# A fused spectral filter and gated MLP on one core: the forward token transform from fp16 halves, an opening with fp32 transposes, and a re-timed planner

## The chip, the cores and the metric

The kernel runs on one core of a Trainium2 chip. Its engines are PE (TensorE: matmuls; its weight loads are shown apart, as PEld), DVE (VectorE), ACT (ScalarE), POOL (GpSimd) and SP (SyncE, which issues the transfers). The metric is the device time of one execution in microseconds. The kernel before takes 434.8 us, the median of three runs (433.99 to 435.23).

## The reference

The input `x` has 2048 tokens of 448 features. Two branches read its layer norm, and both are added to `x`:

```python
xn = layernorm(x)                            # over the 448 features
A  = irfft2(rfft2(xn) * (w_r + 1j * w_i))    # over tokens and features
g  = relu(xn @ W_gate)                       # 448 -> 1792
B  = (g * (xn @ W_up)) @ W_down              # 1792 -> 448
return x + A + B
```

All of it is fp32. The kernel multiplies in fp16 and keeps the precision by splitting a number in a high and a low half (`hi = fp16(a)`, `lo = fp16(a - hi)`); a product then takes three matmuls, hi·hi, hi·lo and lo·hi.

## The kernel before

**The MLP.** The 1792 hidden features are 14 tiles f of 128, taken in three groups of 5, 5 and 4; the tokens are four chunks q of 512 (order 0, 2, 1, 3). `gu_unit(f, q)` makes gate and up of one tile and chunk: 20 matmuls of 128x512 and two of half the rows, from the weight halves `wt` and the transposed layer norm `T`. Behind it `gu_post` runs `gu_relu` (ACT), `gu_times` (DVE, the instruction g<-gu,g), `gu_hi` (ACT) and `gu_lo` (DVE, h<-g,h). After all tiles of a group and chunk, `dn_mm` multiplies h by W_down (128x448 matmuls into the banks dn). These two are the stream of PE. Two pairs of PSUM banks serve the gu units by turns, so DVE has about one unit's time, after the unit's last matmul, to read its bank.

**The weights.** A tile of W_gate/W_up is loaded (wst<-in_wgu), squared and summed on ACT (junk<-wst), summed over the partitions on POOL (wm), turned into a power of two on DVE (eg, wsc), and split into wt: the high half on ACT (`w_hi`), the low half on DVE (`w_lo`).

**The spectral branch** is the background, listed in `bg` with a DVE cost for each step. Forward, in eight passes: `f_dft` (features; 48 small matmuls), an eviction by ACT, `f_fold`, `f_a` and `f_b` (butterflies on DVE over a buffer in the tile arena), `f_sdft` (tokens: a 64-point transform by four fp32 matmuls of 64x64 weights and 464 columns, one in each quadrant of PE's array, L824), an eviction `f_y`, and `f_y1`. Then come butterflies over the tiles y (`stage2` to `stage4`), the multiplication by the filter, and the way back, whose runs on PE are `i_sdft` and `i_ddft`. A background run uses PE in another form than the stream does.

**The opening.** For chunk 0 the layer norm has to be transposed on PE before anything else can start. `ln_xn` makes xn in fp32; `ln_hi` (ACT) and `ln_lo` (DVE) split it into halves; `ln_tp` transposes three 128x128 tiles of each half, for four token tiles; `ln_ev` evicts them to T (rows 0 to 2 high, 5 to 7 low); `ln_tpc` transposes the remaining 64 features in 24 pieces for the rows 3, 4 and 8. While the data comes, `keep_warm` runs matmuls on zeros (16, and 4 more later). Chunks 2, 1 and 3 are transposed by DMA.

**The order.** Every call is recorded by `Order` and placed by `Order.place` (all instructions therefore carry the line L416 of the profile). The opening is fixed by hand: each engine takes its own pieces in the order of the string OPENING (L34). From there on `place` picks for each engine, by a table of costs (`cost`, `matmul`, `dma`, ISSUE, SLACK, SOON), among the nodes that are ready; the stream keeps its order, and a background run is put in when it is ready and has waited longer than its hold (HOLDS, L28), or when the stream's next matmul is not ready. An instruction of DVE counts as free for a dependent one at its end plus 0.04 us, and the engine for another one 0.083 us ahead of its end (ISSUE). `run_bg` gives the background out over the units from RAMP to LASTGU before the last, and BACK says how many units early it may start.

Of the kernel before, what the change touches and what calls it, by code (L numbers as in the profile page):

```python
# [34 lines left out]
lx0 lx4 bn0 lx12 bn4 lx8 lw ag0 lid lw ag4 sqA raA rbA rcA warm rdA rmA xn0 bn12 bn8 an4 ag12 hi0 ag8 lo0 hi4 sqB tpA0  # L35
wsqW0g0 lx14 lw tpB0 raB lo4 rbB rcB tpB4 kw4 rdB rmB aevA0 wsqW0g1 lw xn8 tpA4 parW0g0 wexW0g0 lx6 lw vevB4 hi8 vevB0
hi12 wscW0g0 vevA4 whiW0g0 lx10 tpA8 aevA8 tpA12 parW0g1 lo8 tpB8 wsqW1g1 hh00 hl00 wsqW1g0 lw lw lw xn12 vevA12 hh01
lo12 wexW0g1 wloW0g0 parW1 wscW0g1 tpB12 whiW0g1 vevB12 lx2 tpC aevC1 bn6 lwd3 lh01 lh00 wexW1 wscW1 vevB8 hh10 vevC0
whiW1g0 wloW0g1 hl10 wloW1g0 whiW1g1 wloW1g1 hl11 bn10 bn2 bn14 hh11 lwd0 wsqW3g1 ml0 ml1 wsqW2g0 wsqW2g1 lh11 wsqW3g0
parW2 lfd ag2 hl01 ag10 lh10 ag14 ag6 hp0 re0 tm0 lw lwd1 sqC raC wexW2 lw gu1g0 rbC wscW2 rcC rdC xn14 parW3 wexW3  # L40
whiW2g1 wloW2g1 lwd4 gu1g1 hi14 cp14 wscW3 xn2 whiW2g0 lo14 wloW2g0 whiW3g0 hi2 lwd2 whiW3g1 wsqW4g0 xn10 re1 wsqW4g1
parW4 wloW3g0 hi10 cp2 ly0 tm1 gu2g1 gu2g0 cp10 ly4 wdq0 wdq4 wloW3g1 wexW4 gh0 xn6 wdq3 lo10 hp2 gu3g0 hi6 re2 ly12
wscW4 whiW4g0 lo2 whiW4g1 gu3g1 lo6 wdq2 gh1 tm2 dm14 wdq1 gl0 wloW4g0 gu4g0 ly8 dm10 wloW4g1 gl1 cp6 gu4g1 re3 gh2
tm3 wdp wdsc gh3 gl3 aevC2 wdh1 dm2 gl2 wdl1 wdh4 dm6 wdh3 wdl4 hp4 re4 wdl3 tm4 wdh0 wdl0 wdh2 wdl2 gh4 gl4
# [3 lines left out]
LASTGU = 9  # L48
# [56 lines left out]
def _constants():  # L105
# [54 lines left out]
    c_fm = c_fm.reshape(2, 4, 128, 2, 64).transpose(1, 2, 0, 3, 4)  # L160
    ident = np.eye(128, dtype=np.float16)
# [21 lines left out]
class Order:  # L183
# [3 lines left out]
    ISSUE = dict(V=-0.083, A=-0.098, G=-0.06)  # L187
    SOON = 0.2
    SWITCH = 0.093
    SLACK = 0.8  # L190
# [85 lines left out]
    def cost(self, eng, op):  # L276
        name, k, n = op.call[0].__name__, op.call[2], max(op.n)
        if eng == "G":
            return 0.47 + 0.16 * (op.n[0] > 2) * (op.n[0] - 2) if "reduce" in name else 0.2 + 2e-3 * n
        ap = any(c == 1 for c in op.n[1:]) and n > 8  # L280
        if eng == "V":
            return 0.15 + 1.04e-3 * n + 0.06 * ap
        dark = op.out[1].space == bass.MemoryType.PSUM
        return 0.22 + 8e-4 * n - 0.04 * dark + 0.08 * ap + 0.09 * ("accum_out" in k)

    def matmul(self, op):
        o, w, x = op.out
        rows, cols = w.ap[0][1], op.n[1]
        r, c = w.offset // w.ap[0][0], o.offset // o.ap[0][0]
        half = (64, 64 if cols <= 64 else 128) if rows <= 64 else (128, 128)  # L290
        quads = [(i, j) for i in ((0, 1) if rows > 64 or x.dtype == F32 else (r // 64,))
                 for j in ((0, 1) if half[1] == 128 else (c // 64,))]
        return half, quads, 0.42 if x.dtype == F32 else op.n[0] / 2400 + 0.0025

    def dma(self, op):
        o, i = op.out
        if "transpose" in op.call[0].__name__:
            return 1.37, 1.78, 1.55
        z = o.ap[0][1] * op.n[0] * (4 if o.dtype == F32 else 2)
        dram = isinstance(i.tensor, bass.DRamTensorHandle)  # L300
        return 0.47 if dram else 0.63, 2.0 if dram else 1.7, z * 2.8e-6

    def place(self):
# [14 lines left out]
        def lag(op):  # L318
            pe = op.node.eng == "P"
            far = 0.04 if op.node.eng == "S" or op.node.fixed else self.SLACK  # L320
            return max([d.end + (far if d.node.eng == "S" else 0.04) for d in op.deps
                        if not (pe and d.node.eng == "P")], default=0.0)
# [20 lines left out]
        def pick(e):  # L343
# [6 lines left out]
            if e != "P":  # L350
                t = [est(n) for n in r]
                lo = min(t) + self.SOON
# [5 lines left out]
            run = min(runs, key=lambda v: (v[1] > free["P"] + self.SOON, v[0].key)) if runs else None  # L358
# [7 lines left out]
            if self.matmul(head.ops[0])[0][0] == 64 and h[1] <= now + self.SOON:  # L366
                return h
# [53 lines left out]
def tile_gfnet_reglu(ctx: ExitStack, tc: tile.TileContext, x, xr, wgu, wd, wf, ident, c_fd, c_fm, c_im, c_row, c_id,  # L421
                     out):
    nc = tc.nc
    order = Order()
    V, A, P, G, Q = (order.engine(e, eng) for e, eng in zip("VAPGS", (nc.vector, nc.scalar, nc.tensor, nc.gpsimd, nc.sync)))
# [106 lines left out]
    id_t = ft([128, 128], F16, "id_t")  # L532
# [46 lines left out]
    def load_fm(q):  # L579
        t = ft([128, 2, 2, 64], F32, "fm", 4)  # L580
# [55 lines left out]
    for t in tts:  # L636
        G.memset(t[:, 3:9:5, 64:128], 0.0)
# [41 lines left out]
    def ln_lo(n2):  # L679
# [41 lines left out]
    def ln_ev(n2, part, act):  # L721
        q, j = n2 % 4, n2 // 4
        copy(Tq[q][:, 5 * part:5 * part + 3, 128 * j:128 * (j + 1)], tp[n2, part][:, 0:3], act)

    def ln_tpc(q):

        b = (fx(), fx())
        for i in range(3):
            tp["end", i] = b[i // 2].bitcast(F16)[:, 512 * (i % 2):512 * (i % 2) + 512]
        for j in range(4):  # L730
            t = tt[q + 4 * j].rearrange("p a b -> p (a b)")
            c, l = t[:, 384:448], t[:, 1024:1088]
            for i, half in enumerate(((c, t[:, 7:512:8]), (l, c), (l, t[:, 647:1152:8]))):
                for h in range(2):
                    P.transpose(tp["end", i][64 * h:64 * h + 64, 128 * j:128 * j + 128], half[h], id_t)

    def ln_evc(q, i, act):
        copy(Tq[q][:, (3, 4, 8)[i], :], tp["end", i], act)
# [38 lines left out]
    def f_dft(a, b):  # L777

        ps, T = fx2(), Tq[a % 4]
        with order.run(HOLDS[0]):  # L780
# [32 lines left out]
    def f_part(a, n2):  # L813
        k = int(n2 != a)
        return Fq[a][:, :, :, KC * k:KC * (k + 1)].rearrange("p s c k -> p c s k")

    def f_hi(a, n2):
        Xh[n2] = ft([128, 2, 2, NG, KC], F16, "Xh", 2)
        A.activation(Xh[n2][:, 0], f_part(a, n2), AF.Copy)

    def f_lo(a, n2):
        V.tensor_tensor(Xh[n2][:, 1], f_part(a, n2), Xh[n2][:, 0], op=OP.subtract)

    def f_sdft(a):  # L824
        w, ps = fm_t[a], fx2()
        sfx[a] = ps
        with order.run(HOLDS[1]):
            for k in range(2):
                for b in range(2):
                    p, q = slice(64 * k, 64 * k + 64), slice(64 * b, 64 * b + 64)  # L830
                    P.matmul(ps[q, k, 0:XW], w[p, b], f_part(a, a + 8 * b)[p], start=True, stop=True,
                             skip_group_check=True)
# [199 lines left out]
    def row_dft(d):  # L1032
        y = state["rowps"] = fx()[:, 0:NG * KC]
        with order.run(HOLDS[0]):
# [79 lines left out]
    def i_sdft(p):  # L1114
        ps = fx2()
        sps[p] = ps
        with order.run(HOLDS[2]):
# [33 lines left out]
    def i_ddft(a, b):  # L1151
# [6 lines left out]
        with order.run(HOLDS[3]):  # L1158
# [225 lines left out]
    PE_US = {"f_dft": 0.85, "f_sdft": 0.75, "i_sdft": 0.85, "i_ddft": 0.82, "row_dft": 0.2}  # L1384
# [42 lines left out]
    for k, a in enumerate(seq):  # L1427
# [3 lines left out]
        add(2.2, f_b, a)  # L1431
        if k < 7:
# [176 lines left out]
    def keep_warm(n):  # L1609
        for i in range(n):  # L1610
            P.matmul(wps[i % 2], warm[:, 0:128], warm, start=True, stop=True)
# [3 lines left out]
              **{f"kw{n}": (lambda n=n: keep_warm(n)) for n in (4,)},  # L1615
# [6 lines left out]
    for c, q in enumerate(CHUNKS[:2]):  # L1622
# [4 lines left out]
        for j in range(4):  # L1627
            n2 = q + 4 * j
            for tag, fn, *a in (("lx", load_xr), ("ly", load_x), ("bn", ln_bn, j), ("ag", ln_ag, j), ("xn", ln_xn),
                                ("hi", ln_hi, c == 0), ("cp", ln_copy), ("lo", ln_lo), ("dm", ln_dma),  # L1630
                                ("tpA", ln_tp, 0), ("tpB", ln_tp, 1)):
                piece(f"{tag}{n2}", fn, *((q,) if tag in ("bn", "ag") else (n2,)), *a)
            for act in range(2):
                piece(f"{'va'[act]}evA{n2}", ln_ev, n2, 0, bool(act))
                piece(f"{'va'[act]}evB{n2}", ln_ev, n2, 1, bool(act))
    q = CHUNKS[0]
    piece("tpC", ln_tpc, q)
    for i in range(3):
        for act in range(2):
            piece("va"[act] + f"evC{i}", ln_evc, q, i, bool(act))  # L1640
# [41 lines left out]
    wps = dn_bank(), dn_bank()  # L1682
# [119 lines left out]
```

## Time and profile before

| what | us |
|---|---|
| median of three runs | 434.8 |
| the profiled execution | 434.42 |
| its span, first to last instruction | 432.6 |

The profile lists busy time by engine, the chain of waits that ended last, groups of instructions alike in engine, tiles and form (count, busy us, mean ns of one, then the idle time ahead of them and who ended it), and rows in order of time. A recorded duration of PE includes the pipeline, so that two matmuls that follow each other overlap in it: the distance of two starts is what one costs. The same holds for DVE, where an instruction may start before the recorded end of the one ahead.

### The profile page before, as it was taken

Reading aid. Unit: us, or ns where it says so; the run is one execution under the profiler, and the core shown is the slowest. Engines: PE = TensorE matmul, PEld = TensorE weight load, DVE = VectorE, ACT = ScalarE, POOL = GpSimd, SP = SyncE. Lnnn points to the kernel's source line nnn. Section 1 sums busy time; section 2 is a strip of 40 time slices with the busy share of each in tenths; the row PEclk is TensorE's granted clock in tenths of the full one; section 3 lists DMA queues with packets and bytes.
Section 4 is the critical chain, followed back from the end, with each engine's and each line's share of the span. In section 5 each row is a group of like instructions: output and inputs, shape, how many; then the busy total and the mean of one; then the engine's idle time right before and its main releaser. Section 6 shows DMA issues by size and latency. Waiting matters only on the chain.

```text
span 432.6 us, 8471 instructions
## 1 busy us (share of the span) xinstructions
PE 425.2 (98%) x3222; PEld 202.8 (47%) x3222; DVE 384.0 (89%) x804; ACT 262.7 (61%) x495; POOL 30.1 (7%) x72
## 2 busy tenths in 40 slices
PE   7999999999999999999999999999999999999996
PEld 3644544444444445445444444444554554545554
DVE  6998989999988899999999999999999999993443
ACT  5898466387447938645534634763666765864661
POOL 1140013042001100000000110100000000000000
PEclk9999999999999999999999999999999999999999
DMA  8859319009104703343504300040222121310212
GB/s 258 300 120 258 137 44 233 16 7 218 58 3 131 232 14 113 89 123 84 153 18 104 99 1 0 2 95 8 51 53 45 49 75 24 94 44 2 85 45 86
DMA packets 37721, 38.63 MB, mean 89 GB/s; under 512 B 18928, under 2 KB 33072, under 8 KB 37680
## 3 DMA queue, kind: packets, MB, share of 16 engines
q1 hardware_dynamic: 37680, 38.09, 31.9%
q8 instruction: 25, 0.41, 0.4%
q14 instruction: 16, 0.13, 0.1%
HBM read 23.20 MB, written 3.67 MB: 62 GB/s over the span
## 4 chain that ended last, share of the span: by engine, by line
DVE 47%; PE 34%; ACT 6%; issue 5%; DMA 4%; SPq 3%; DVEq 0%; POOL 0%; ACTq 0%
PE gu L416 23%; DVE y L416 19%; DVE arena L416 13%; PE dn L416 8%; DVE g L416 5%; DVE h L416 4%; PE fx L416 3%; SPq L416 3%; DVE wst L416 2%; ACT arena L416 2%; DVE wt L416 2%; DMA arena<-in_wf 1%; ACT h L416 1%; DMA wst<-in_wgu 1%; ACT y L416 1%
## 5 line engine op out<-in xcount | busy, mean ns | idle before, releaser
L416 PE MATMUL gu<-T,wt 128*128 128x512 f16 (+2 forms) x1250 | 264.4, 376 | 0.0
L416 PEld LDWEIGHTS <-wt 128*128 128x128 f16 (+1 forms) x1250 | 111.4, 97 | 144.0 <-issue 21.6
L416 PE MATMUL dn<-wdt,h 128*128 128x448 f16 x648 | 125.8, 353 | 0.6 <-ACT dn L416 0.5
L416 PEld LDWEIGHTS <-h 128*128 128x128 f16 x684 | 66.0, 98 | 61.8 <-issue 2.6
L416 ACT ACTIVATE h<-g 128x512 f16<-128x512 f32 x56 | 35.1, 628 | 54.5 <-DVE g L416 54.3
L416 DVE TENSOR_TENSOR y<-y 128x464 f32<-128x464 f32 (+2 forms) x82 | 58.8, 745 | 2.3 <-ACT y L416 1.5
L416 DVE TENSOR_TENSOR arena<-arena 128x116 f32<-128x116 f32 (+6 forms) x105 | 52.9, 525 | 4.3 <-ACT arena L416 2.8
L416 ACT ACTIVATE g<-gu 128x512 f32<-128x512 f32 x56 | 32.8, 586 | 34.0 <-PE gu L416 33.9
L416 DVE SCALAR_TENSOR_TENSOR g<-gu,g 128x512 f32<-128x512 f32 x56 | 38.3, 684 | 16.5 <-ACT g L416 13.4
L416 DVE TENSOR_TENSOR h<-g,h 128x512 f16<-128x512 f32 x56 | 38.4, 688 | 4.5 <-ACT h L416 3.8
L416 ACT ACTIVATE xy<-dn,dsc 128x448 f32<-128x448 f32 x44 | 27.5, 625 | 21.0 <-PE dn L416 20.5
L416 DVE TENSOR_TENSOR wst<-wst 128x116 f32<-128x116 f32 (+2 forms) x96 | 30.7, 375 | 0.7
L416 DVE SCALAR_TENSOR_TENSOR y<-y 128x232 f32<-128x232 f32 (+2 forms) x52 | 30.0, 599 | 0.5
L416 ACT ACTIVATE dn<-xy,dinv 128x448 f32<-128x448 f32 x44 | 27.8, 636 | 1.4 <-DMA xy<-in_x 0.3
L416 PEld LDWEIGHTS <-arena 64*128 64x128 f16 (+2 forms) x836 | 17.3, 96 | 14.3 <-issue 6.2
L416 DVE SCALAR_TENSOR_TENSOR wt<-wst,wsc,wt 128x512 f16<-128x512 f32 x28 | 20.2, 745 | 2.3 <-ACT wt L416 2.2
L416 ACT ACTIVATE arena<-arena 128x116 f32<-128x116 f32 (+3 forms) x33 | 15.0, 465 | 10.7 <-DMA arena<-in_wf 7.5
L416 POOL PARTITION_ALL_REDUCE wm<-wm x15 | 8.8, 588 | 175.0 <-DVE y L416 94.3
L416 ACT ACTIVATE wt<-wst,wsc 128x512 f16<-128x512 f32 x28 | 19.0, 711 | 1.8 <-DVE wsc L416 1.8
L416 POOL COPY arena<-arena 128x56 f16<-128x56 f16 (+1 forms) x36 | 15.9, 474 | 59.7 <-ACT arena L416 53.8
L416 ACT ACTIVATE junk<-wst 128x512 bf16<-128x512 f32 x28 | 17.4, 622 | 1.9 <-DMA wst<-in_wgu 1.5
L416 PE MATMUL fx<-arena 64*128 64x64 f16 (+3 forms) x484 | 17.8, 245 | 0.7 <-DVE T L416 0.5
(81 smaller groups left out, 294.2 us busy)
## 6 DMA issues: line engine op xcount, KB each, us to landing
wst<-in_wgu SPq DMA_DIRECT2D x28, 256.0 KB, 4.7
arena<-in_wf SPq DMA_DIRECT2D x16, 232.0 KB, 3.2
arena<-y SPq DMA_DIRECT2D x64, 58.0 KB, 2.0
arena<-wst SPq DMA_DIRECT2D x32, 116.0 KB, 2.3
y<-in_xr SPq DMA_DIRECT2D x16, 224.0 KB, 4.5
xy<-in_x SPq DMA_DIRECT2D x16, 224.0 KB, 4.1
out<-xy SPq DMA_DIRECT2D x15, 224.0 KB, 2.0
wdst<-in_wd SPq DMA_DIRECT2D x14, 224.0 KB, 3.3
```

The costliest lines, as they stand in the source:

```text
L416: fn(*a, **k)
```

## The change

`f_sdft` works from fp16 halves: two new background steps, `f_hi` (ACT) and `f_lo` (DVE), split the 928 columns of a pass, its constants c_fm are stored as halves, and each pass has twelve fp16 matmuls of 464 columns where it had four fp32 ones. In the opening xn is transposed in fp32 straight from `ln_xn` (the identity is fp32 too), 12 transposes and 8 plain matmuls by the identity where there were 24 transposes and 24 pieces; the halves are made on the way out of PSUM (`ln_th` on ACT, `ln_tl` on DVE), and half of row 4 is copied by a DMA. OPENING is written anew, with 10 and later 7 matmuls to keep warm. In the planner the cost of DVE is measured again, the waiting times HOLDS are one number for each of 34 runs, an ACT instruction counts 0.2 us after DVE, SOON is one number for each engine, and RAMP, BACK, WSOON, SLACK and LASTGU change.

```diff
-AHEAD, RAMP = 3, 6
-NWARM = 16
+AHEAD, RAMP = 3, 5
+NWARM = 10
-HOLDS = 3.0, 3.0, 3.0, 3.0
-BACK = 2
-EVAC, POST, WSOON = 6, 8, 4
+HOLDS = (2, 6, 2, 3, 3, 8, 3, 3, 8, 3, 5, 4, 2, 3, 8, 8, 8, 10, 5, 3, 0.5, 8, 3, 0.5, 10, 5, 0.5, 3, 5, 3, 2, 3, 6, 3)
+SOON = dict(P=0.2, V=0.1, A=0.15, G=0.2, S=0.3)
+LATE = 0.2
+BACK = 3
+EVAC, POST, WSOON = 6, 8, 3
...
-LASTGU = 9
+LASTGU = 6
...
-    ISSUE = dict(V=-0.083, A=-0.098, G=-0.06)
+    ISSUE = dict(V=-0.079, A=-0.098, G=-0.06)
-    SLACK = 0.8
+    SLACK = 1.3
...
-            return 0.15 + 1.04e-3 * n + 0.06 * ap
+            return 0.155 + 1.042e-3 * n + 0.06 * ap
...
+    def ln_th(n2, act):
+        js = slice(128 * (n2 // 4), 128 * (n2 // 4) + 128)
+        copy(Tq[n2 % 4][:, 0:3, js], tp[n2], act)
+    def ln_tl(n2):
+        T, js = Tq[n2 % 4], slice(128 * (n2 // 4), 128 * (n2 // 4) + 128)
+        V.tensor_tensor(T[:, 5:8, js], tp[n2], T[:, 0:3, js], op=OP.subtract)
...
+        tp["end"] = side[1]
+        for j, x in enumerate(xts):
+            js = slice(128 * j, 128 * j + 128)
+            for h, c in ((0, slice(384, 448)), (1, slice(7, 512, 8))):
+                P.matmul(tp["end"][64 * h:64 * h + 64, js], x[:, c], id_t, start=j == 0, stop=True,
+                         skip_group_check=True)
+    def ln_end(q, i, act=False):
+        T, a = Tq[q], tp["end"]
+        if i == 0:
+            copy(T[:, 3, :], a, act)
+        elif i == 1:
+            Q.dma_start(T[64:128, 4, :], T[0:64, 3, :])
...
+    def f_hi(a):
+        Xh[a] = ft([128, 2, NG, 2, 2 * KC], F16, "Xh", 2)
+        A.activation(Xh[a][:, 0].rearrange("p s c k -> p (s c k)"), Fq[a].rearrange("p s c k -> p (s c k)"), AF.Copy)
+    def f_lo(a):
+        x, h = (t.rearrange("p s c k -> p (s c k)") for t in (Fq[a], Xh[a][:, 0]))
+        V.tensor_tensor(Xh[a][:, 1].rearrange("p s c k -> p (s c k)"), x, h, op=OP.subtract)
...
+            for i, (h, c) in enumerate(((1, 0), (0, 0), (0, 1))):
+                for k in range(2):
+                    for b in range(2):
+                        p, q = slice(64 * k, 64 * k + 64), slice(64 * b, 64 * b + 64)
+                        x = Xh[a][p, h, :, :, KC * b:KC * (b + 1)].rearrange("p s c k -> p c s k")
+                        P.matmul(ps[q, k, 0:XW], w[p, c, b], x, start=i == 0, stop=i == 2, skip_group_check=True)
```

The first place is PE at the end of the opening of the kernel before: the first matmuls of the MLP (gu_93 from T and wt_91) are followed by transposes (arena to gu_86 and fx).

```order
L416 MATMUL gu_93<-T_63,wt_91 128x256
L416 LDWEIGHTS arena [waits DVE_49]
L416 MATMUL gu_86<-arena 128x128
L416 LDWEIGHTS arena
L416 MATMUL gu_86<-arena 128x128
L416 LDWEIGHTS arena
L416 MATMUL gu_86<-arena 128x128
L416 LDWEIGHTS arena
L416 MATMUL fx<-arena 64x128
```

The same place of the changed kernel; dn_85 is the bank of the matmuls that keep PE warm, dn_83 that of the eight matmuls of the remaining features (an fp32 matmul shows no weight load of its own in these rows).

```order
L420 MATMUL dn_85<-arena 128x512
L420 MATMUL gu_87<-arena 128x128 [waits DVE_49]
L420 MATMUL gu_87<-arena 128x128 x2
L420 MATMUL fx<-arena 128x128 [waits DVE_49]
L420 MATMUL fx<-arena 128x128 x2
L420 MATMUL dn_83<-arena 64x128 x8
L420 LDWEIGHTS wt_91 [waits Activation_49]
L420 MATMUL gu_94<-T_63,wt_91 128x256 [waits Activation_49]
```

All transposes now stand ahead of the first matmul of the MLP, and none behind it.

The second place is DVE in the third pass of the forward token transform of the kernel before: the second half of `f_fold` (arena<-y), the butterflies `f_a` and `f_b` (arena<-arena), and gu_times and gu_lo (g, h) among them. A row that waits for DVE_49 waits for an earlier row of its own engine.

```order
L416 TENSOR_TENSOR arena<-y 128x16x29 [waits DVE_49]
L416 TENSOR_TENSOR arena<-arena 128x2x232 [waits DVE_49]
L416 TENSOR_TENSOR arena<-arena 128x2x2x116 [waits DVE_49]
L416 TENSOR_TENSOR arena<-arena 128x3x116 [waits DVE_49]
L416 SCALAR_TENSOR_TENSOR g_104<-gu_86,g_104 128x512 [waits PE_49,Activation_49]
L416 TENSOR_TENSOR arena<-arena 128x3x116
L416 TENSOR_TENSOR arena<-arena 128x116 [waits DVE_49]
L416 TENSOR_TENSOR h_123<-g_104,h_123 128x512 [waits Activation_49]
L416 TENSOR_TENSOR arena<-arena 128x2x2x58 [waits DVE_49] x2
L416 TENSOR_TENSOR arena<-arena 128x116
```

The same pass in the changed kernel; the row of 128x928 is the new `f_lo` of the pass ahead.

```order
L420 TENSOR_TENSOR arena<-y 128x16x29 [waits DVE_49]
L420 TENSOR_TENSOR arena<-arena 128x928 [waits Activation_49]
L420 TENSOR_TENSOR arena<-arena 128x2x232 [waits DVE_49]
L420 SCALAR_TENSOR_TENSOR g_105<-gu_87,g_105 128x512 [waits PE_49,Activation_49]
L420 TENSOR_TENSOR arena<-arena 128x2x2x116 [waits DVE_49]
L420 BN_AGGR arena<-arena 128x2
L420 TENSOR_TENSOR arena<-arena 128x3x116 [waits DVE_49]
L420 TENSOR_TENSOR arena<-arena 128x3x116
```

Between the rows of the chain that need the row just ahead there now stand rows of other work. Over the whole program 201 DVE instructions wait for the instruction directly ahead of them before the change, and 103 after it (counted by the values of the semaphore that each waits for); the number of DVE instructions goes from 804 to 808, that of ACT's ACTIVATE from 436 to 440.

More of the change, by code (lines that the diff above doesn't have):

```diff
@@ L319, in lag @@
             pe = op.node.eng == "P"
-            far = 0.04 if op.node.eng == "S" or op.node.fixed else self.SLACK
-            return max([d.end + (far if d.node.eng == "S" else 0.04) for d in op.deps
-                        if not (pe and d.node.eng == "P")], default=0.0)
+            e = op.node.eng
+            far = dict(S=0.04 if e == "S" or op.node.fixed else self.SLACK)
+            if e == "A" and not op.node.fixed:
+                far["V"] = LATE
+            return max([d.end + far.get(d.node.eng, 0.04) for d in op.deps if not (pe and d.node.eng == "P")],
+                       default=0.0)
         def open_(n):
@@ L357, in pick @@
                 return None
-            run = min(runs, key=lambda v: (v[1] > free["P"] + self.SOON, v[0].key)) if runs else None
+            run = min(runs, key=lambda v: (v[1] > free["P"] + SOON["P"], v[0].key)) if runs else None
             if head is None:
@@ L365, in pick @@
             now = max(free["P"], max(bank.values()))
-            if self.matmul(head.ops[0])[0][0] == 64 and h[1] <= now + self.SOON:
+            if self.matmul(head.ops[0])[0][0] == 64 and h[1] <= now + SOON["P"]:
                 return h
@@ L579, in load_fm @@
     def load_fm(q):
[L580 removed]
+        t = ft([128, 2, 2, 2, 64], F16, "fm", 4)
         Q.dma_start(t, c_fm[q])
@@ L719, in copy @@
             V.tensor_copy(o, i)
-    def ln_ev(n2, part, act):
-        q, j = n2 % 4, n2 // 4
-        copy(Tq[q][:, 5 * part:5 * part + 3, 128 * j:128 * (j + 1)], tp[n2, part][:, 0:3], act)
-    def ln_tpc(q):
[L727 to L738, printed above, removed]
+    def ln_th(n2, act):
[4 more added lines that the diff above has]
+        V.tensor_tensor(T[:, 5:8, js], tp[n2], T[:, 0:3, js], op=OP.subtract)
+    def ln_tpc(q):
+        tp["end"] = side[1]
[10 more added lines that the diff above has]
+            Q.dma_start(T[64:128, 4, :], T[0:64, 3, :])
+        elif i == 2:
+            V.tensor_tensor(T[0:64, 4, :], a[0:64], T[0:64, 3, :], op=OP.subtract)
+        else:
+            V.tensor_tensor(T[:, 8, :], a, T[:, 3, :], op=OP.subtract)
     fi, sfx = {}, {}
@@ L779, in f_dft @@
         ps, T = fx2(), Tq[a % 4]
-        with order.run(HOLDS[0]):
+        with order.run(hold()):
             for k, n2 in enumerate((a, b)):
@@ L826, in f_sdft @@
         sfx[a] = ps
[L827 to L832, printed above, removed]
+        with order.run(hold()):
+            for i, (h, c) in enumerate(((1, 0), (0, 0), (0, 1))):
[4 more added lines that the diff above has]
+                        P.matmul(ps[q, k, 0:XW], w[p, c, b], x, start=i == 0, stop=i == 2, skip_group_check=True)
     def rotate(t, b, p, sgn):
@@ L1033, in row_dft @@
         y = state["rowps"] = fx()[:, 0:NG * KC]
-        with order.run(HOLDS[0]):
+        with order.run(hold()):
             for a in range(2):
@@ L1116, in i_sdft @@
         sps[p] = ps
-        with order.run(HOLDS[2]):
+        with order.run(hold()):
             for b in range(2):
@@ L1157, in i_ddft @@
             A.activation(sides[e], xy2[:, a, :, 224 * e:224 * (e + 1)], AF.Copy, scale=fsc[:, 2:3])
-        with order.run(HOLDS[3]):
+        with order.run(hold()):
             for k, n2 in enumerate((a, b)):
@@ L1431, in tile_gfnet_reglu @@
         add(2.2, f_b, a)
+        add(0.0, f_hi, a)
+        add(1.12, f_lo, a)
         if k < 7:
@@ L1610, in keep_warm @@
         for i in range(n):
-            P.matmul(wps[i % 2], warm[:, 0:128], warm, start=True, stop=True)
+            P.matmul(wps, warm[:, 0:128], warm, start=True, stop=True)
     pieces = {"lid": lambda: Q.dma_start(id_t, ident), "lfd": lambda: Q.dma_start(fd_t, c_fd),
               "lw": load_wn,  "warm": lambda: keep_warm(NWARM),
-              **{f"kw{n}": (lambda n=n: keep_warm(n)) for n in (4,)},
+              **{f"kw{n}": (lambda n=n: keep_warm(n)) for n in range(1, 9)},
               "wdp": lambda: wd_sum(len(groups[0])),
@@ L1681, in tile_gfnet_reglu @@
     G.memset(warm, 0.0)
-    wps = dn_bank(), dn_bank()
+    side[1], side[2] = dn_bank(), fx()
+    wps = dn_bank()
     side[0] = gu_bank()
```

103 lines of the change are left out of this document (45 added, 58 removed).

## The prediction

> **What bounds the kernel now.** I read the page's busy times and its chain first, then the chain in order of time, the waits of PE, and the busy times by stage.
>
> ```profile
> span 432.6 us, 8471 instructions
> PE 425.2 (98%) x3222; PEld 202.8 (47%) x3222; DVE 384.0 (89%) x804; ACT 262.7 (61%) x495; POOL 30.1 (7%) x72
> DVE 47%; PE 34%; ACT 6%; issue 5%; DMA 4%; SPq 3%; DVEq 0%; POOL 0%; ACTq 0%
> ```
>
> The chain names DVE more often than PE, but PE is busy 98% of the span. Which of them sets the time is read from whether PE runs at its peak and whether it ever waits.
>
> ```profile
> 322.88 9.28 PE gu L416 x44
> 338.00 9.19 PE dn L416 x48
> ...
> PE dn L416 <- POOL arena L416: 1.9, 1, 1.9
> PE gu L416 <- DVE arena L416: 1.0, 3, 0.5
> PE dn L416 <- ACT dn L416: 0.5, 1, 0.5
> ```
>
> The first two rows are pieces of the chain (start, us): 44 gu matmuls in 9.28 are 0.211 us each for 512 columns, 48 dn matmuls in 9.19 are 0.191 for 448. The last three are PE's longest waits: 1.9 before the very first matmul, 1.0 in the opening, 0.5 later on. So PE streams at one pace from the opening to the end and hardly waits: **the time is the opening, plus PE's work, plus a tail**. DVE matters where it would make PE wait.
>
> ```profile
> 20.00:120.00 100.00, 100.00 (x818) 45.84 (x817) 93.99 (x220) 66.37 (x129) 19.82 (x42) 1.00 0.49 123
> 120.00:150.00 30.00, 30.00 (x199) 13.62 (x198) 24.80 (x51) 21.76 (x44) 1.87 (x8) 1.00 0.43 131
> 150.00:313.00 163.00, 162.87 (x848) 74.48 (x847) 159.00 (x292) 87.78 (x184) 5.40 (x10) 1.00 0.24 63
> ...
> 380.00:420.00 40.00, 40.00 (x464) 20.35 (x464) 20.22 (x36) 25.28 (x38) 0.00 (x0) 1.00 0.13 47
> ```
>
> The columns are length, then PE, PEld, DVE, ACT and POOL busy. From 20 to 313 us DVE is idle 6.0 + 5.2 + 4.0 = 15.2 us, after 380 it is half idle. It is nearly as full as PE, so each microsecond added to it has to be found somewhere.
>
> **Part 1: f_sdft in halves, on PE.**
>
> ```profile
> 55.10 1.02 PE L416 MATMUL fx<-arena 64*64 64x464 f32 x8
> 56.05 0.60 PE L416 MATMUL gu<-T,wt 128*128 128x512 f16 x2
> L416 PE MATMUL fx<-arena 64*64 64x464 f32 x64 | 8.1, 577 | 0.0
> ```
>
> One fp32 pass takes 56.05 - 55.10 = 0.95 us. It is eight instructions of 0.577 us within 1.02, so the four quadrants work side by side. Twelve fp16 matmuls of 464 columns are then three rounds of four; a round by the dn row is 464/448 x 0.191 = 0.198, three are 0.59. I add 0.04 for the change of the array's form, 0.63, and save 0.32 in each of eight passes: **-2.6 us**. The ends: 0.59 gives -2.9; if fp16 quadrants ran only two at a time (no row shows 64x64 fp16), six rounds are 1.19, which gives +1.9. I stay near the three rounds, since the fp32 row shows four quadrants at once. The stream keeps its matmuls and its number of changes of form, so the runs that move among it add nothing themselves.
>
> The Trainium skill ("FP8 and Floating Point Precision", TensorE Precision Notes) counts a true fp32 matmul as four passes through the array. By that rule three fp16 rounds would be three quarters of 0.95, and the term -1.9 in place of -2.6. The trace speaks for more: four rounds of 0.198 would be 0.79, and the row shows 0.95.
>
> **Part 2: the same on DVE and ACT.**
>
> ```profile
> L416 DVE TENSOR_TENSOR y<-y,arena 128x928 f32<-128x928 f32 x16 | 18.0, 1122 | 0.4
> L416 ACT ACTIVATE arena<-wst,fsc 128x928 f16<-128x928 f32 x8 | 8.7, 1090 | 3.0 <-DVE wst L416 3.0
> 52.27 0.65 DVE arena L416
> 52.94 0.65 DVE arena L416
> 229.64 1.19 DVE L416 TENSOR_TENSOR y<-y 128x464 f32<-128x464 f32 x2
> ```
>
> f_hi adds 8 x 1.09 = 8.7 us to ACT, which is busy 61%; I cost it at nothing, hidden beside PE's stream (uncovered, a pass would be 1.1 us later). f_lo adds 8 x 1.12 less the overlap of 0.08, **8.3 us on DVE**. Against it stands the order. Butterflies of 464 columns that need each other start 0.67 apart (52.27 to 52.94); two that don't take 1.19 together, so the second starts 0.55 after the first. Needing the instruction directly ahead costs 0.12 us. The orders have 201 such instructions before and 103 after: 98 x 0.12 = **11.8 us off DVE**. Its sum is -3.5 us, about as much as PE gains in all, so DVE should stay as far behind PE as today, even if it idled its 15.2 us again. Term for the time: 0. The ends are in the rivals. Later in the program the background reaches three gu units further (LASTGU), where DVE is half idle; that costs nothing.
>
> **Part 3: the opening.**
>
> ```profile
> 1.89 6.11 PE L416 MATMUL dn<-arena 128*128 128x512 f16 x16 [1.89 <-POOL arena L416]
> ...
> 12.38 1.15 PE L416 MATMUL gu<-T,wt 128*128 128x256 f16 x9
> ...
> 13.77 1.38 PE L416 MATMUL fx<-arena 128*64 128x128 f16 x24
> ...
> 15.08 7.22 PE L416 MATMUL gu<-T,wt 128*128 128x256 f16 x47
> ```
>
> Before, nine matmuls of the MLP (1.15) ran at 12.38, then transposes, and the stream flows from 15.08. Were it in one piece it would begin at 15.08 - 1.15 = 13.9. In the changed order it is in one piece, behind the last transposes. When can these run?
>
> ```profile
> 2.61 0.43 SPq L416 DMA_DIRECT2D wst<-in_wgu  x1
> wst<-in_wgu SPq DMA_DIRECT2D x1, 256.0 KB, 4.8
> ...
> 5.46 0.75 DVE L416 SCALAR_TENSOR_TENSOR arena<-arena 128x2 f32<-128x2 f32 x4
> 6.12 0.51 DVE L416 TENSOR_SCALAR y<-y,arena 128x448 f32<-128x448 f32 x1
> 7.83 0.33 PE L416 MATMUL fx<-arena 128*128 128x128 f16 x3
> 8.21 0.28 ACT L416 ACTIVATE arena<-arena,eps 128x2 f32<-128x2 f32 x1
> 8.40 0.61 ACT L416 ACTIVATE junk<-wst 128x512 bf16<-128x512 f32 x1
> 11.29 0.71 ACT L416 ACTIVATE wt<-wst,wsc 128x512 f16<-128x512 f32 x1
> ...
> L416 DVE TENSOR_TENSOR wst<-wst 128x348 f32<-128x348 f32 x16 | 8.0, 517 | 0.2
> L416 PEld LDWEIGHTS fx<-arena 64*64 64x64 f32 x64 | 1.7, 131 | 3.2 <-issue 2.8 <-ACT g L416 0.4
> ```
>
> The first weights land at 2.61 + 4.8 = 7.4. On ACT their squares (0.61) now stand ahead of the second root (0.28): 8.3. Behind it DVE has six small instructions of 0.75/4 = 0.19, one ln_tl (0.52, as 348 columns) and two normalisations (0.51): 8.3 + 1.1 + 0.5 + 1.0 = 10.9. Then PE has three fp32 transposes and eight fp32 matmuls, two of them side by side: seven steps. One is at least the fp16 transpose (0.33 for three, 0.11) and at most 128/464 of an fp32 pass, 0.26, with two uncovered weight loads of 0.131: 0.52. I take 0.26, nearest to the fp32 row: 1.8. With 0.3 for the pipeline and ACT's evictions the stream begins at **13.0** (ends: 11.9 and 14.8). The high half of the weights came 2.9 us after its squaring began (8.40 to 11.29) and takes 0.71; from 7.4 on that is 11.0, in time. So **-0.9 us** (-2.0 to +0.9).
>
> ```profile
> arena<-wst SPq DMA_DIRECT2D x32, 116.0 KB, 2.3
> ```
>
> Added on SP: half of T's row 4 is now copied by a DMA behind an eviction (issued near 13.7); its reader stands 36 half-width matmuls (36 x 0.11 = 3.9 us) into the stream, at 16.9. By this row it lands 2.3 us later, in time; by the opening's 4.8 it comes at 18.5 and PE waits 1.6. I take **+0.3**. Queued behind it on SP are token loads for chunk 2, needed much later.
>
> **Sum**, against the profiled execution's 434.42 (the median is 0.4 higher): -2.6 - 0.9 + 0 + 0.3 = -3.2, **431.2 us**.
>
> **The rivals.**
>
> *The opening gives nothing.*
>
> ```profile
> 4.42 0.15 PEld L416 LDWEIGHTS <-arena 128*128 128x128 f16 x1 [0.28 <-issue]
> 4.85 0.15 PEld L416 LDWEIGHTS <-arena 128*128 128x128 f16 x1 [0.28 <-issue]
> 9.45 1.03 PE L416 MATMUL dn<-arena 128*128 128x512 f16 x4
> ```
>
> Warm-up matmuls start 0.43 us apart at first (4.42, 4.85), but four take 1.03 later: PE's pace doubles after some 5 us of work. Now 11 instead of 16 run before the first wait; at 0.43 they end near 6.6, and xn0 or the identity holds PE for about 1 us. If the pace then doubles only later, the five warm-up matmuls ahead of the last transposes cost 5 x 0.21 = 1.1 more, and seven slow steps 1.8 more. Half of these 2.9, or the late copy's 1.6, makes up for the 0.9: about 432.9. For it: the gap; against it: 11 matmuls still last 4.7 us. Chance 0.18.
>
> The Trainium skill ("TensorE: Matmul & The Clock Gate", Part 1, What's actually happening) gives the rule behind this: the clock is released after one busy window of about 3.4 us, and windows run free of the program's start. By it 4.7 us are enough only where a window falls well, and otherwise the release is one window later; the trace, where it came 5 us after the first matmul, agrees.
>
> *DVE takes PE's place (the slower case).* The mechanism is f_lo's 8.3 us in the stretch to 313 us, with the order's saving not realised because the rows put in between wait for ACT themselves. With half the saving (5.9) DVE falls 8.3 - 5.9 + 3.2 = 5.6 us further behind a PE that is 3.2 ahead. The two pairs of banks allow one unit, 22 x 0.21 = 4.6; PE loses at least 1.0: 432.2 or more, chance 0.08. With none of it, 11.5 - 4.6 = 6.9 is lost: **438.1**, chance 0.05. It is slower than before from a loss of 3.2 on, that is where less than 3.7 of the 11.8 is saved. For it: DVE at 97% from 150 to 313. Against it: the 15.2 us of idle time, and BACK = 3, which lets the background start earlier.
>
> *f_sdft does not gain.* Two quadrants at a time: +1.9 in place of -2.6, 435.7. Chance 0.05.
>
> **How the numbers follow.** The forecast has 0.64, and its own range is 429.2 (both first terms at their better end) to 432.6 (a copy 1.6 late). Left out above 434.4 are the last two cases, 0.10, and a little below 429: the range is 429.0 to 434.4. About 0.3%, 1.3 us, is what a measurement of this kernel can tell from no change. Faster: the forecast's 0.64, and two thirds of the 0.26 in between, 0.81. Within: the rest of these, 0.09. Slower: 0.10.
>
> **What would show it.** In the changed profile the f_sdft passes should be twelve matmuls within 0.6 to 0.7 us, gu matmuls should start near 13.0 and not pause, DVE's busy time should fall by some 3 us in spite of eight new rows of 928 columns, and PE's waits after 20 us should stay below 1 us. I am wrong if PE waits for g or h (DVE is the bound), if the first 256-column matmuls start after 14, or if 0.2-us steps become 0.43 there.

## The result and the profile after

The changed kernel takes **430.8 us** (median of six runs, 429.2 to 431.4) against 434.5 for the kernel before on the same chip. The ratio is 0.9912, with a 95% interval from 0.9894 to 0.9929: faster by 0.9%. The forecast was 431.2. The profiled execution took 430.66, where that of before took 434.42.

The page of the changed kernel begins so:

```profile
span 428.9 us, 8505 instructions
PE 421.4 (98%) x3231; PEld 202.6 (47%) x3231; DVE 382.9 (89%) x808; ACT 266.0 (62%) x499; POOL 31.8 (7%) x80
...
PE 93%; DMA 3%; DVE 1%; ACT 1%; issue 0%; SPq 0%; DVEq 0%; ACTq 0%
```

PE is 3.8 us shorter, about what the span lost. The chain (last line) now runs through PE for 93% of the span; before, DVE held 47% of it. Nothing but PE's own work lies between the opening and the end, apart from one transfer that comes back below (the 3% are this one and the load of the first weights, in the opening). The busy times by stage (length, then PE, PEld, DVE, ACT, POOL) and PE's waits of the same execution:

```profile
20.00:120.00 100.00, 99.26 (x838) 46.61 (x837) 95.03 (x218) 71.46 (x133) 20.59 (x42) 1.00 0.53 128
120.00:150.00 30.00, 30.00 (x219) 13.70 (x218) 27.91 (x70) 26.01 (x50) 3.11 (x11) 1.00 0.36 119
150.00:313.00 163.00, 163.00 (x851) 75.10 (x849) 160.39 (x291) 88.45 (x184) 4.46 (x6) 1.00 0.25 66
```

```profile
PE dn L420 <- DMA arena<-in_ident: 1.1, 1, 1.1
...
PE gu L420 <- DVE wt L420: 0.7, 1, 0.7
```

DVE idles 5.0 + 2.1 + 2.6 = 9.7 us before 313 us (15.2 in the kernel before). After 20 us PE waits once, 0.74 us in the first stretch, for the low half of a weight tile (wt). The 0.3 us near 173 us and the 0.6 us near 313 us that the kernel before lost are gone; the second of them was this row (the starts are 0.6 later than the pace would have them):

```profile
313.49 3.00 PE L416 MATMUL dn<-wdt,h 128*128 128x448 f16 x15 [0.46 <-ACT dn L416]
```

Where did the time come from? I lined up both traces by the amount of MLP work that PE had finished and read how far the changed kernel was ahead: 1.57 us at 20 us, 0.76 behind the wait at 26 us, 0.92 at 33 us, 3.1 at 176 us (behind all eight f_sdft passes), 3.7 from 370 us on. The parts add up: 0.9 of the opening, 1.7 of f_sdft (0.21 in each pass, below), 0.3 and 0.6 of the two waits, and 0.2 because PE's array changes its form 91 times after 20 us in place of 93. I count as a change two matmuls in a row whose rows name different forms (128\*128, 64\*128, 64\*64); each costs some 0.1 us, since the 512-column matmul ahead of one starts 0.31 before the next matmul and not 0.21.

### The profile page after: what moved, and what is told of

It reads as the page before. It is cut to its first block, busy times and chain, and to the rows that moved or that the text cites. A ratio compares the mean times of both kernels' runs of the same rounds, so it can differ in the third digit from the quotient of the medians.

```text
span 428.9 us, 8505 instructions
## 1 busy us (share of the span) xinstructions
PE 421.4 (98%) x3231; PEld 202.6 (47%) x3231; DVE 382.9 (89%) x808; ACT 266.0 (62%) x499; POOL 31.8 (7%) x80
## 4 chain that ended last, share of the span: by engine, by line
PE 93%; DMA 3%; DVE 1%; ACT 1%; issue 0%; SPq 0%; DVEq 0%; ACTq 0%
PE gu L420 59%; PE dn L420 29%; PE fx L420 6%; DMA wst<-in_wgu 3%; DVE wt L420 1%; SPq L420 0%; ACT junk L420 0%; DVE arena L420 0%; ACT wt L420 0%; ACT arena L420 0%; DVE T L420 0%; ACT T L420 0%; DVE xy L420 0%; DVE y L420 0%; DVE wsc L420 0%
## 5 line engine op out<-in xcount | busy, mean ns | idle before, releaser
L420 DVE TENSOR_TENSOR arena<-arena 128x116 f32<-128x116 f32 (+7 forms) x113 | 61.2, 566 | 7.4 <-ACT arena L420 6.6
L420 ACT ACTIVATE arena<-arena 128x116 f32<-128x116 f32 (+4 forms) x41 | 22.3, 561 | 4.9 <-DVE arena L420 3.4
L420 PEld LDWEIGHTS <-arena 64*128 64x128 f16 (+2 forms) x881 | 16.2, 96 | 14.1 <-issue 8.1
L420 POOL COPY arena<-arena 128x56 f16<-128x56 f16 (+1 forms) x36 | 16.8, 508 | 59.4 <-ACT arena L420 56.0
L420 DVE TENSOR_TENSOR y<-y,arena 128x928 f32<-128x928 f32 x16 | 17.9, 1118 | 0.3
```

Of the source, the lines that this page charges most:

```text
L420: fn(*a, **k)
```

## The experiments

SOON, in some of the names, is the planner's tolerance for "can start about now"; it is explained below. Not all rows ran on one chip, but each ratio is to the kernel before on the same chip.

| kernel | us | ratio to before, 95% interval |
|---|---|---|
| changed kernel | 430.84 | 0.9912 (0.9894 to 0.9929) |
| fp16 f_sdft alone on the kernel before | 436.46 | 1.0041 (1.0026 to 1.0056) |
| new planner alone | 433.43 | 0.9979 (0.9970 to 0.9989) |
| new opening alone | 434.94 | 1.0018 (1.0005 to 1.0030) |
| change without fp16 f_sdft | 432.22 | 0.9942 (0.9926 to 0.9958) |
| change without the new planner | 436.40 | 1.0054 (1.0027 to 1.0082) |
| the same with SOON of DVE 0.1 | 431.80 | 0.9948 (0.9933 to 0.9963) |
| change with SOON of DVE 0.2 | 445.68 | 1.0249 (1.0231 to 1.0267) |
| change with two loads earlier on SP | 429.67 | 0.9886 (0.9870 to 0.9902) |

Two of the three parts are slower alone, and the third brings 0.2%. Together they bring 0.9%.

### f_sdft from fp16 halves, alone

The diff's lines for c_fm, `load_fm`, `f_hi`, `f_lo` and `f_sdft` on the kernel before, and nothing else.

> The kernel before with f_sdft from fp16 halves (f_hi and f_lo added) and nothing else of the change: old opening, old planner. DVE has 204 instructions that need the one directly ahead, as before. Theory: the new order on DVE is what pays for f_lo. Without it DVE gets 8.3 us more in the stretch to 313 us and PE, 1.7 us shorter by eight passes, runs ahead of it: 8.3 + 1.7 - 4.6 (one unit of the banks) = 5.4 us of new waits, about 434.5 - 1.7 + 5.4 = 438. Rival: DVE's 15.2 us of idle time before 313 us takes f_lo in, no new wait: 434.5 - 1.7 = 432.8.

436.5, between the two. PE's part is there: each pass takes 0.74 in place of 0.95. The order of this kernel near 300 us, PE's rows:

```profile
302.46 11.51 PE L416 MATMUL dn<-wdt,h 128*128 128x448 f16 x60
313.91 0.87 PE L416 MATMUL fx<-arena 64*128 64x64 f16 x48
```

The same place in the kernel before:

```profile
303.44 3.00 PE L416 MATMUL dn<-wdt,h 128*128 128x448 f16 x15
306.37 0.87 PE L416 MATMUL fx<-arena 64*128 64x64 f16 x48
307.18 5.85 PE L416 MATMUL dn<-wdt,h 128*128 128x448 f16 x30
```

The rows of 48 are the first `i_sdft`, with which the way back begins. It stood behind 15 dn matmuls; now it stands behind all 60, 7.5 us later: f_lo's 8.3 us, seen where they come out. PE does not lose these 7.5 us there, since it has dn matmuls to run. It pays at three other places (waits of the fp16-alone kernel as the profile counts them, then the rows of the second and the first of them):

```profile
PE fx L416 <- ACT xy L416: 1.3, 1, 1.3
PE fx L416 <- DVE arena L416: 1.3, 1, 1.3
PE gu L416 <- DMA T<-arena: 0.7, 1, 0.7
```

```profile
320.99 0.79 PE L416 MATMUL fx<-idc_t,arena 64*128 64x56 f16 x48 [1.25 <-DVE arena L416]
...
430.02 1.31 PE L416 MATMUL fx<-wdt,h 128*128 128x224 f16 x12 [1.31 <-ACT xy L416]
```

The first `i_ddft` (321 us) stands too close behind the late `i_sdft`, and PE waits 1.25 us for DVE between them. The last one has been pushed against the end: twelve dn matmuls need its bank and stand 1.3 us until ACT has emptied it, where 27 other matmuls ran in between before. By the starts of PE's rows the three places cost 0.9 (at 76 us), 1.4 and 1.5, together 3.8. Against them the kernel before loses 0.9 at 173 and 313 us, which this one does not. And the array changes its form 101 times in place of 93, 0.8 more. -1.7 + 3.8 - 0.9 + 0.8 is +2.0, which is what the two profiled executions differ by (436.40 and 434.42; the medians by 1.8). So DVE did take PE's place, but on the way back and at the end, not by the banks in the stretch to 313 us.

### One number of the planner

```diff
-SOON = dict(P=0.2, V=0.1, A=0.15, G=0.2, S=0.3)
+SOON = dict(P=0.2, V=0.2, A=0.15, G=0.2, S=0.3)
```

> The changed kernel with one number of the planner put back, SOON of DVE 0.2 in place of 0.1; 201 of DVE's instructions then need the one directly ahead (103 in the changed kernel). Theory: this number makes the order that saves about 98 x 0.12 = 11.8 us on DVE; without them DVE is the bound in the stretch to 313 us and PE loses 11.8 - 4.6 = 7 us: about 438. Rival: DVE's 9.7 us of idle time between 20 and 313 us takes most of it in, and the time stays within 1 us of 430.8.

445.7, 15 us slower, more than either expectation. Among the instructions that could start within SOON of the earliest one, the planner takes the first of its list. One that needs the instruction directly ahead starts 0.12 us later than another. With SOON 0.2 that is "as good", and the planner takes it; with 0.1 it first puts in something that does not depend. Hence 201 or 103 such instructions. Up to 313 us PE loses no more here than in the changed kernel but for 1.2 us at 75 us. The loss is all at the end, in the chain and the stage:

```profile
402.73 1.24 DVE arena L420
...
404.01 1.32 PE fx L420 x48
...
405.41 1.17 ACT xy L420 x2
...
406.62 1.47 PE fx L420 x48
```

```profile
380.00:420.00 40.00, 31.84 (x408) 17.04 (x407) 21.58 (x40) 23.65 (x35) 0.00 (x0) 0.87 0.16 49
```

PE, ACT and DVE hand the passes of the way back to each other with nothing in between; PE stands still for 8 us of 40, and its granted clock falls to 0.87 in that stage. Why 15 us here and only 3.5 in the run before, with the first `i_sdft` as late in both (314.5 and 313.9)? The other numbers of the planner differ (HOLDS above all, but also LATE, BACK, LASTGU and the rest), and waiting times that were found for one order need not fit another. None of them was tried alone, so this stays open.

### The old planner under the rest of the change, and SOON alone

All numbers of the planner as before (first kernel), then SOON of DVE 0.1 and nothing else of the new planner (second):

```diff
-SOON = dict(P=0.2, V=0.2, A=0.2, G=0.2, S=0.2)
+SOON = dict(P=0.2, V=0.1, A=0.2, G=0.2, S=0.2)
```

> The changed kernel with the planner's numbers of before (HOLDS 3.0 throughout, SOON 0.2, no LATE, BACK 2, WSOON 4, LASTGU 9, RAMP 6, the old costs); fp16 f_sdft and the new opening stay. 203 of DVE's instructions need the one ahead. Theory after the two runs with some 200 of them: DVE's lateness does not stop PE in the stretch to 313 us, it starts the way back (the first i_sdft at 314 in place of 306 us) late, and PE runs out of other work near the end. That costs here what it cost the fp16 form alone on the old planner, less the opening's 0.9: 436.5 - 0.9 = 435.6. Rival: SOON alone decides, the rest of the planner is worth nothing: 445, as with SOON 0.2 in the changed kernel.

> The same kernel with one number more of the new planner: SOON of DVE 0.1 in place of 0.2, all else of the planner as before. 117 instructions need the one ahead. Theory: this number brings the first i_sdft back to about 307 us and with it nearly the whole gain: 431 to 432. Rival: the 34 waiting times and the other numbers are needed as well: 434 or more.

436.4 (435.6 expected) and 431.8: the theory held both times. One number is worth 4.6 us between the medians, most of the planner's part; the 34 waiting times and the rest bring the last 0.5 to 1.0 (the changed kernel took 430.8 and, on another chip, 431.3). The six runs with SOON 0.2 lie between 435.0 and 439.0, and the profiled one is the fastest of them: the two traces account for 3.4 of the 4.6, and what made the other runs longer is not known. PE's rows with SOON 0.2:

```profile
300.98 11.51 PE L420 MATMUL dn<-wdt,h 128*128 128x448 f16 x60
312.42 0.87 PE L420 MATMUL fx<-arena 64*128 64x64 f16 x48
```

and with 0.1:

```profile
301.02 3.00 PE L420 MATMUL dn<-wdt,h 128*128 128x448 f16 x15
303.95 0.87 PE L420 MATMUL fx<-arena 64*128 64x64 f16 x48
304.76 8.99 PE L420 MATMUL dn<-wdt,h 128*128 128x448 f16 x45
```

The stream is at the same point in both (301.0), and the way back begins 8.5 us earlier: 86 fewer dependent instructions (203 and 117) by 0.12 would be 10.3.

### The planner alone, the opening alone, and the change without fp16

> The kernel before with the new planner's numbers alone (old opening, fp32 f_sdft): 112 instructions need the one ahead, 201 before. Theory: DVE has room before 313 us as it is, so 10 us less on it is worth only the two waits of PE that the trace of before shows (0.3 at 173 us, 0.6 at 313 us): 434.7 - 0.9 = 433.8, with the first i_sdft some 8 us earlier than 306.4. Rival: without f_lo the free DVE is worth more (an earlier way back shortens the end): 432.5 or less. A third: waiting times that were found for other runs fit badly here and cost 1 to 10 us.

433.4, 0.7 below the kernel before on the same chip, where the theory had 0.9; the waits at 173 and 313 us are gone. The other half of the theory missed: DVE has 10 us less to do and the first `i_sdft` still starts at 306.0 us (306.4 before), behind 15 dn matmuls, not 8 us earlier. Without f_lo DVE was on time already, and time that nobody waits for is worth nothing.

> The kernel before with the new opening alone (old planner, fp32 f_sdft). Theory: the stream is 1.6 us ahead at 20 us and gives 0.8 back at the wait near 26 us, and keeps the rest: 434.7 - 0.8 = 433.9. Rival: DVE, no faster than before, starts the way back no earlier than 306 us and the end takes the gain back: 434.7.

434.9 in the median, so the rival's time came out. The trace shows only part of it: the profiled execution is the fastest of ten (433.88; the slowest took 436.2). In it the stream was 2.2 us ahead at 20 us. It gave 0.7 back at 74 us, stood 1.4 us at 311 us where the kernel before stands 0.6, and ended 0.5 ahead. What the slower runs lost besides is not shown. Its waits:

```profile
PE dn L420 <- ACT dn L420: 1.3, 1, 1.3
...
PE gu L420 <- DMA T<-arena: 0.5, 1, 0.5
```

The kernel with the new planner alone has neither wait, nor has the changed kernel. So the new planner is what lets PE keep its early start; which of the late steps ahead of these two waits it mends was not tried.

> The changed kernel with f_sdft in fp32 again, so without f_hi and f_lo; new opening and new planner stay. Theory from the two traces: eight passes of 0.95 in place of 0.74, +1.7 us, and the 8.3 us that DVE loses are worth nothing: 432.5. By the prediction's own term (0.95 against 0.63) it would be +2.6: 433.4. Rival: DVE without f_lo frees PE elsewhere and gives part of it back: 431 to 431.5.

432.2: fp16 in f_sdft is worth 1.4 us once the planner makes room for f_lo, near the 1.7 of the traces and well under the 2.6 of the prediction. From 33 us on the two profiled executions differ by 1.9: 1.7 of f_sdft and 0.2 of two changes of form (93 here, 91 in the changed kernel). DVE without f_lo gave nothing more.

### The wait at 26 us

Behind the opening the chain of the changed kernel holds one transfer:

```profile
16.44 6.01 DMA wst<-in_wgu
27.08 9.88 PE gu L420 x48
```

SP takes its transfers in the order of the string OPENING. Its rows there:

```profile
7.68 2.29 SPq L420 DMA_DIRECT2D wst<-in_wgu  x4
13.25 0.56 SPq L420 DMA_DIRECT2D T<-T  x1
13.85 1.07 SPq L420 DMA_DIRECT2D y<-in_xr  x2
14.96 0.91 SPq L420 DMA_DIRECT2D wdst<-in_wd  x2
15.91 0.43 SPq L420 DMA_DIRECT2D xy<-in_x  x1
16.44 0.38 SPq L420 DMA_DIRECT2D wst<-in_wgu  x1
```

and one of ACT's, with what it waited for:

```profile
22.54 0.63 ACT L420 ACTIVATE junk<-wst 128x512 bf16<-128x512 f32 x1 [0.82 <-DMA wst<-in_wgu]
```

From 10.0 to 13.25 SP stands still: the copy of row 4 (T<-T) waits for its eviction, and the first half of the fifth weight tile, whose buffer was free near 11.5, is five transfers behind it. It lands at 22.5. ACT waits 0.82 us for it, and the high half of the fourth tile, next on ACT, its low half on DVE and PE's matmul are late by as much. The edit moves two tokens of OPENING:

```diff
-lw lh11 end1 lx14 hl11 lh10 hl10 ml0 z0 lx10 bn10
+lw lh11 lw end1 lx14 hl11 lh10 hl10 ml0 z0 lx10 lw bn10
-lwd2 ly4 z1 lw ag14
+lwd2 ly4 z1 ag14
-rcC lw rdC
+rcC rdC
```

> The changed kernel with two instructions moved on SP: the load of the fifth weight tile's first half ahead of the copy of row 4 (issued then near 11.5 us, where it was issued at 16.4), its second half behind the two token loads that follow (near 15, was 17.4). Theory: the 0.8 us that PE waits near 26.3 us for the low half of a weight tile comes from SP standing behind the copy; ACT waits 0.82 us for that load and is late by as much. The wait goes: 430.0. Rival: the wait is held by DVE's or ACT's own work ahead of these halves and stays: 430.8. A third case: the copy comes later behind the load, and PE waits at 16.5 instead: 431.2.

429.7, and the wait is gone. PE has no idle time left in that stage (busy times of this kernel), and from 27 us to the end its stream is 0.9 us ahead of the changed kernel's:

```profile
20.00:120.00 100.00, 100.00 (x840) 46.82 (x839) 95.70 (x220) 71.34 (x134) 21.10 (x42) 1.00 0.52 127
```

> The kernel with the two loads moved on SP once more, beside the changed kernel on the same chip. Theory: 0.9 us less than the changed kernel (its stream was 0.86 us ahead from the wait near 26 us to the end). Rival: the difference between the two was one of chips, and they agree within 0.3.

> The changed kernel as it is, the partner of the run above on the same chip: 430.8, and in its trace again the wait of 0.8 us near 26 us for the low half of a weight tile.

Side by side on one chip: 429.66 (429.44 to 429.90) and 431.27 (429.79 to 431.66), ratios to before 0.9882 (0.9868 to 0.9897) and 0.9915 (0.9902 to 0.9929). The version with the two loads moved beats both kernels, and its runs lie closer together. The wait was there again in the changed kernel (0.94 us). The medians differ by 1.6, not by the 0.9 expected. In the profiled executions 0.7 of that is a stream that began late in the changed kernel, as the next section shows; whether the other runs began so is not known.

### PE's pace in the opening

> The changed kernel with 3 instead of 10 matmuls in the first block that keeps PE warm; PE then works from 2.0 to about 3.7 us and stands still until the first transposes at 8. The prediction's rival: the pace doubles only after some 5 us of nearly unbroken work, so the transposes, the five warm-up matmuls behind them and the first 256-column matmuls run at half pace until about 13 us; the stream starts 1 to 2 us later (13.5 to 14.5) and partly at 0.22 a step: 432 to 433. The other theory: the pace is back after any stretch of work of a few us, the opening's chain is DVE's and ACT's, and PE's pace there is hidden: stream from 12.6, 430.8.

431.7, ratio 0.9933 (0.9917 to 0.9950). That lies between the two theories, and the start of the stream (13.40) just short of the rival's 13.5. The picture of the pace is clear:

```profile
1.97 1.89 PE L420 MATMUL dn<-arena 128*128 128x512 f16 x4 [1.97 <-POOL arena L420]
8.14 1.30 PE L420 MATMUL dn<-arena 128*128 128x128 f32 x4 [4.28 <-DVE arena L420]
9.23 0.85 PE L420 MATMUL gu<-arena 128*128 128x128 f32 x3
9.87 1.76 PE L420 MATMUL dn<-arena 128*128 128x512 f16 x5
11.47 0.49 PE L420 MATMUL gu<-arena 128*128 128x128 f32 x3
13.40 6.91 PE L420 MATMUL gu<-T,wt 128*128 128x256 f16 x50
```

Three transposes take 0.85 at 9.23 and 0.49 at 11.47; the starts in the trace go from 0.21 to 0.11 apart near 10.9. The stream starts at 13.40, 0.87 later than in the first profile of the changed kernel, and at 28 us both are level: the late start only used up the wait at 26 us. (The load of the fifth weight tile was issued late as well, at 17.32, but landed 4.8 us later, where in the first profile of the changed kernel it took 6.0.) What this does to the median (0.5 us above its neighbour on the chip, with intervals that overlap) is not settled.

The unchanged program showed the same thing by itself. In the run beside it, of the changed kernel as it is, PE's rows were

```profile
7.51 1.30 PE L420 MATMUL dn<-arena 128*128 128x128 f32 x4 [0.67 <-DVE arena L420]
8.60 0.84 PE L420 MATMUL gu<-arena 128*128 128x128 f32 x3
...
11.32 0.49 PE L420 MATMUL gu<-arena 128*128 128x128 f32 x3
...
13.24 0.94 PE L420 MATMUL gu<-T,wt 128*128 128x256 f16 x7
```

while the first profile of it had

```profile
7.96 0.73 PE L420 MATMUL dn<-arena 128*128 128x128 f32 x4 [1.12 <-DMA arena<-in_ident]
8.54 0.49 PE L420 MATMUL gu<-arena 128*128 128x128 f32 x3
```

after the same eleven warm-up matmuls (1.97 to 6.85): full pace from the first transpose in one execution, half pace until 11 us in the other. Here the late start was not made up for: SP's copy of row 4 and with it the fifth weight tile were late too (issued at 17.18, landed at 23.4), PE waited 0.94 us for it, and the stream stayed 0.9 us behind the first profile to the end. Of nine profiles with this warm-up, two started at half pace, this one and that of the change without fp16 f_sdft. In the latter the late start used up the wait at 26 us, as it did with 3 matmuls.

> The kernel with the two loads moved on SP and 12 in place of 10 matmuls in the first block that keeps PE warm, so that it ends near 7.5 in place of 6.6 us. In the changed kernel's second look PE was still at half pace at the first transposes (0.213 each) and the stream started 0.7 us late; in its first look it was at full pace (0.11). Theory: whether the pace has doubled by then hangs on how far the warm-up reaches; with two more it always has, the stream starts near 12.3, and no run is above 430: 429.5. Rival: the two matmuls hold PE while the first tile could be transposed, 0.3 us later: 429.9 or more.

429.75 (429.54 to 429.98), no different from ten warm-up matmuls (429.66). The profiled execution was at full pace at the first transpose (7.65 us) and the stream began at 12.2. One profile cannot show that it always is; the two matmuls cost nothing and bought nothing that can be measured.

## Why the prediction was right, and where not

**The bound** (opening, PE's stream, tail) was right: PE's work, its few waits and the opening account for the 3.7 us.

**The sum came out within 0.4 us partly by luck.** Against the profiled execution it was -2.6 - 0.9 + 0 + 0.3; the runs show -1.7 for f_sdft, -0.9 for the opening with its copy, 0 for DVE, and -1.1 that the sum did not have. Two of its bounds are also added up wrongly: both first terms at their better end give 429.8 (434.42 - 2.9 - 2.0 + 0.3), not 429.2, and the copy 1.6 late gives 432.5, not 432.6. By its own terms the rival of the opening comes to 432.5 or 432.7, not 432.9.

**Part 1, f_sdft on PE: mis-sized.** The prediction had 0.95 to 0.63 and -2.6; the page and the trace give 0.95 to 0.74, eight times 0.21: **-1.7**. The passes of the changed kernel:

```profile
56.34 0.81 PE L420 MATMUL fx<-arena 64*64 64x464 f16 x12
57.08 2.12 PE L420 MATMUL gu<-T,wt 128*128 128x512 f16 x9
```

The rounds of four start at 56.34, 56.57 and 56.77 in the trace, and the stream follows at 57.08: 0.23, 0.20 and 0.31. Three rounds of 0.2 leave some 0.14 at the two changes of form, where I allowed 0.04. (Another 0.10 lies ahead of the pass, in the matmul before it; it is there with fp32 too and does not enter the difference.) The same 0.14 belongs to the fp32 pass. Its two sets of four rows start 0.45 apart and the stream follows 0.50 behind the second; two neighbouring rounds of the fp16 pass take 0.43 at the front and 0.51 at the back. So 0.95 less 0.14 is 0.81, four rounds of 0.2. So the step that failed is "four rounds of 0.198 would be 0.79, and the row shows 0.95": the difference was the change of form, not a slower fp32. The rule of the Trainium skill ("FP8 and Floating Point Precision", TensorE Precision Notes), that a true fp32 matmul is four passes, would have given -1.9; the measurement agrees with it (three quarters of the 0.81, and 0.14, are 0.75).

That the stream keeps "its number of changes of form" was nearly so in the changed kernel (93 before, 91 after), but it is no rule: the two kernels with fp16 f_sdft and the old planner have 101.

**Part 2, DVE 0: right, and for the reason given.** f_lo alone puts the way back 7.5 us later (forecast 8.3), the order brings it forward by 8.5 (forecast 11.8), and in the changed kernel it is in its place (306.1 us, behind 30 dn matmuls in a stream 3 us ahead). The first `i_sdft` of the changed kernel:

```profile
306.10 0.88 PE L420 MATMUL fx<-arena 64*128 64x64 f16 x48
```

f_lo's eight rows:

```profile
L420 DVE TENSOR_TENSOR arena<-arena 128x928 f16<-128x928 f32 x8 | 9.0, 1129 | 2.6 <-ACT arena L420 2.6
```

DVE's busy time fell by 1.1 us only, where I wanted some 3: what an instruction saves that need not wait lies partly in the gap ahead of it, which is not busy time (0.02 of the 0.12 in the butterflies of the prediction, which end at 52.92 and start at 52.94; 98 such gaps are 2 us). The idle time before 313 us fell by 5.5.

**The rival in which DVE takes PE's place** had a price of the right kind (6.9 us lost; 4.6 between the two values of SOON with the old planner, 3.5 for f_lo alone, but 15 with SOON 0.2 in the changed kernel) and the wrong place. PE never waited for g or h. The planner gives the stream's instructions their turn and lets the background fall behind; the debt comes due on the way back, where the stream has too little left to put between two passes. "I am wrong if PE waits for g or h" would not have shown it.

**Part 3, the opening: -0.6 in sum forecast, -0.8 found behind the wait at 26 us (-0.9 from 33 us on), by two errors.** The chain was right step by step: first squares at 7.68 us (7.4 forecast), last normalisation done at 10.81 (10.9), stream from 12.53 (13.0). The 0.3 for pipeline and evictions was too much, so the stream is 1.57 ahead in place of 0.9 (0.8 to 2.2 over the nine profiles with this opening and warm-up). The copy of row 4 was in time and cost nothing itself, where I had +0.3. But "Queued behind it on SP are token loads for chunk 2, needed much later" left out the fifth weight tile: 0.8 us.

**Not in the sum at all:** the waits of the kernel before at 173 and 313 us, 0.9 together, which went with the new planner (which alone brings 0.7), and the two changes of form, 0.2. They made up for the 0.9 by which f_sdft was too good, and that was luck.

**The rival in which the pace doubles late** comes true in some executions (two of nine profiles) and costs 0.7 us at the stream's start. Of that, one execution paid 0.9 at the end, with the weight tile, and the other nothing; the rival's price was about 1.5. The Trainium skill ("TensorE: Matmul & The Clock Gate", Part 1, What's actually happening) has the activity windows run free of the program's start; two executions of one program that differ in just this way agree with it.

**f_sdft does not gain** was wrong: the four quadrants run side by side.

## What to carry to other kernels

A planner's tolerance for "can start about now" must be smaller than the cost that it should avoid: here 0.2 against a gap of 0.12 hid the gap, and one number was worth 4.6 us. Where the critical engine's own stream is served first, lateness of another engine does not show as a wait where it arises but much later, so look at where the pieces of background stand in the stream, not only at who waits. Before an instruction that waits is put on an in-order queue, list all that stands behind it, with the time at which its result is needed.

## What the runs showed of the hardware

An fp32 matmul over four quadrants cost four fp16 rounds (0.81 of 0.95 us). Each change of the array's form cost some 0.1 us: a 512-column matmul starts 0.31 ahead of one in place of 0.21, and a pass of f_sdft is 0.14 longer than its rounds whether it is fp32 or fp16. So the number of changes is a term of its own: 101 in place of 93 is some 0.8 us, an estimate that closes the sum of the fp16 form alone. With SOON 0.2 in the changed kernel PE stood still for 5.5 us (to 404.0); the 48 matmuls behind it took 1.32 us (0.73 at 384 us), and dn matmuls were still 0.37 apart, in place of 0.19, until 411 us: the gap cost some 3 us more than its length (0.6 + 0.6 in the two runs of 48, and ten dn matmuls by 0.18). And whether eleven warm-up matmuls of 0.43 us are enough changed from one execution to the next.
